# Grouped-query decode attention beside a gated MLP: semaphores by hand, one TensorE loop over the heads, two K/V slots, another order of loads

## The chip, the cores and the metric

The kernel runs on one core of one Trainium2 chip. The metric is the device time of one execution in microseconds (us). Before the change it is 682.59 us, the median of three runs (682.55 to 682.78).

## What is computed

A decode step for 8 sequences of one token. The token is normalised, projected to 32 query heads, and attends over a cache of 4096 keys and values in 8 K/V heads of width 128 (four query heads share one). The result is multiplied by a gate from a small MLP and added to the input. All data are float32.

```
xn = layernorm(x)                                       # x: 8 x 1 x 512
q  = (xn @ wq) as 32 heads of 128
s  = softmax(q k^T / sqrt(128)) v, heads joined, @ wo   # k, v: 8 x 8 x 4096 x 128
z  = gelu(xn @ w_in);  z1, z2 = halves of z
g  = silu((z1 * (layernorm(z2) * w_sp + b_sp)) @ w_out)
out = x + s * g
```

K and V are 134 MB each; wq and wo 8.39 MB each; the MLP's weights 5.57 MB.

## The kernel before

The host lays every tensor out as 128 partitions with long rows. K and V come as 32 tiles of 8.39 MB (128 x 16384 floats): for each of the 8 K/V heads two K tiles and two V tiles, each for four of the eight sequences ("half 0" and "half 1"). All large loads go through one ring of three slots of that size and are issued by SyncE's queue (SP), in program order: the MLP's weights (L59), wq (L74), then per head K half 0 and 1 (L289) and V half 0 and 1 (L296). A load waits until the tile that stood in its slot has been read for the last time, and a waiting load holds up the loads behind it in the queue.

At the start VectorE (DVE) normalises x; TensorE (PE) runs the MLP (L144 to L192, with DVE, ScalarE (ACT) and GpSimd (POOL) steps between, up to the gate at L200), while its weights' slot also holds the MLP's intermediate values; then the projection of the queries in two quads of four heads (L207, L213). DVE copies the queries into qz, zero-padded so that 32 columns of a matmul's weights hold one sequence's four query heads at its own place (L219).

Each head: 64 matmuls of scores (L230), 32 for each K tile, accumulate into one PSUM tile of 128 x 1024. The softmax goes over DVE, ACT and four short PE steps (L237 to L258); its result is transposed on PE (L262) and copied zero-padded to pT in 16 small copies (L266). Then 16 value matmuls for each of four pairs of sequences (L275), two pairs for each V tile; DVE multiplies by a mask and reduces (L278, L280), and PE combines (L284).

The last head differs: its second V tile comes in two pieces, behind 12 of wo's 32 blocks (L319), which go into the ring's third slot, and ahead of six pieces with the other 20 (L322). A block is 128 x 512 floats. Blocks 0 to 27 belong to the first seven heads and are multiplied as early as they land (L304, "folding"), the first 12 between the last head's value matmuls. The last head's four blocks are multiplied directly into the output's layout (L351); the folded sum is copied to SBUF (L343) and joined by 8 matmuls (L359). Two DVE steps (L363, L364) and a store (L365) end the program.

The order is made by the Tile framework: it records every tile's readers and writers, sets semaphores itself, and every engine's instructions are written out one after another, all eight heads in full.

Of the kernel before, what the change touches and what calls it, by code (L numbers as in the profile page):

```python
# [1 line left out]

# [11 lines left out]
P = 128  # L14
# [3 lines left out]
G = 4  # L18
# [8 lines left out]
UNIT = 2 * G * 512  # L27
SLOT = HALF * UNIT
W = 64
OUT_ROWS = 2 * B  # L30
WO_EARLY = 12
WO_PIECES = [(12, 20), (20, 26), (26, 28), (28, 30), (30, 31), (31, 32)]
FOLDED = HKV * REP - REP
AHEAD = FOLDED + 2


@with_exitstack
def tile_gqa_gmlp_decode(ctx: ExitStack, tc: tile.TileContext, x, kT, v, wq, wo, w_mlp, out, gate, stored):
    nc = tc.nc
    head = ctx.enter_context(tc.tile_pool(name="head", bufs=1))  # L40
    l = head.tile([P, HKV], F32, name="l")
    nm = head.tile([P, HKV], F32, name="nm")
    neg_half = head.tile([P, 1], F32, name="neg_half")
    diag = head.tile([P, G], F32, name="diag")
    ring = ctx.enter_context(tc.tile_pool(name="ring", bufs=3))
    const = ctx.enter_context(tc.tile_pool(name="const", bufs=1))
    work = ctx.enter_context(tc.tile_pool(name="work", bufs=1))
    small = ctx.enter_context(tc.tile_pool(name="small", bufs=2))
    ps_fix = ctx.enter_context(tc.tile_pool(name="ps_fix", bufs=1, space=bass.MemoryType.PSUM))
    ps = ctx.enter_context(tc.tile_pool(name="ps", bufs=2, space=bass.MemoryType.PSUM))  # L50

    def slot():
        return ring.tile([P, SLOT], F32, name="slot")


    mlp_slot = slot()
    n_in, n_out = NK * 2 * FH, NB * D
    n_mlp = n_in + n_out + P
    nc.sync.dma_start(mlp_slot[:, :n_mlp], w_mlp)  # L59
    w_in_sb = mlp_slot[:, :n_in].rearrange("p (k n) -> p k n", k=NK)  # L60
    w_out_sb = mlp_slot[:, n_in:n_in + n_out].rearrange("p (j d) -> p j d", j=NB)
    side_sb = mlp_slot[:, n_in + n_out:n_mlp]
    spare = [n_mlp]

    def from_slot(rows, n):
        lo = spare[0]
        spare[0] = lo + n
        return mlp_slot[:rows, lo:lo + n]

    x_sb = from_slot(B, D)  # L70
    nc.scalar.dma_start(x_sb, x)

    wq_sb = slot()
    nc.sync.dma_start(wq_sb, wq)  # L74
    wq_sb = wq_sb.rearrange("p (k n) -> p k n", k=NK)


    ident = const.tile([P, P], F32, name="ident")
    make_identity(nc, ident)
    nc.gpsimd.memset(neg_half, -0.5)  # L80
    xnT = const.tile([P, NK, R], F32, name="xnT")
    nc.gpsimd.memset(xnT, 0.0)
    qz = const.tile([P, HKV, B * R], F32, name="qz")
    nc.gpsimd.memset(qz, 0.0)  # L84
    same = const.tile([P, G, R], F32, name="same")
    nc.vector.tensor_reduce(same[:, 0, :], ident.rearrange("p (g r) -> p r g", g=G),
                            op=ALU.add, axis=AX.X)
    for g in range(1, G):
        nc.vector.tensor_copy(same[:, g, :], same[:, 0, :])
    same_all = same.rearrange("p g r -> p (g r)")  # L90
    nc.vector.tensor_reduce(diag, same[:, 0, :].rearrange("p (e g r) -> p g e r", e=2, g=G),
                            op=ALU.add, axis=AX.XY)
    fold = const.tile([P, 2, REP], F32, name="fold")
    nc.vector.tensor_reduce(fold, same[:, 0, :].rearrange("p (e g r) -> p e r g", e=2, g=G),
                            op=ALU.add, axis=AX.X)
    pT = const.tile([P, J, B, 2, G * REP], F32, name="pT")
    nc.gpsimd.memset(pT, 0.0)  # L97
    pick = const.tile([P, 2, R], F32, name="pick")
    nc.vector.memset(pick, 0.0)
    for a in range(2):  # L100
        nc.vector.tensor_copy(pick[:, a, a * B:(a + 1) * B], same[:, 0, :B])

    sc = ps_fix.tile([P, 2, 512], F32, name="sc")
    o_ps = [ps_fix.tile([P, G, DH], F32, name=f"o_ps{i}") for i in range(2)]
    po_ps = ps_fix.tile([P, 2, B * REP], F32, name="po_ps")
    for t in o_ps:
        nc.vector.memset(t, 0.0)

    def scratch(shape, name):
        t = ps.tile([P, 512], F32, name="scr")  # L110
        n = 1
        for s in shape[1:]:
            n *= s
        return t[:shape[0], :n]


    st = small.tile([B, 6], F32, name="st")
    mv = small.tile([B, 2], F32, name="mv")
    rstd = small.tile([B, 2], F32, name="rstd")
    xn = from_slot(B, D)  # L120
    nc.vector.bn_stats(st, x_sb)
    nc.vector.bn_aggr(mv, st)
    nc.vector.tensor_scalar(rstd[:, 0:1], mv[:, 1:2], EPS, None, op0=ALU.add)
    nc.gpsimd.tensor_tensor(rstd[:, 1:2], rstd[:, 0:1], neg_half[:B, 0:1], op=ALU.pow)
    nc.vector.tensor_scalar(xn, x_sb, mv[:, 0:1], rstd[:, 1:2], op0=ALU.subtract, op1=ALU.mult)
    pt = scratch([P, NK * B], "xnT")
    for k in range(NK):
        nc.tensor.transpose(pt[:, k * B:(k + 1) * B], xn[:, k * P:(k + 1) * P], ident[:B, :B])
# [276 lines left out]
```

## Time and profile before

| what | value |
|---|---|
| median of the runs | 682.59 us (682.55 to 682.78) |
| profiled execution, first to last instruction (span) | 680.7 us |
| the difference, which lies around the span | 1.9 us |
| moved by DMA | 291.18 MB, mean 428 GB/s |
| TensorE matmul busy | 360.8 us, 2488 matmuls |
| VectorE busy | 121.5 us, 376 instructions |
| instruction fetches on queue q8 | 19 packets, 0.31 MB |

How to read a profile: "PE" is TensorE's matmuls, "PEld" its weight loads; a float32 matmul of the program stands in the trace as two matmuls and two weight loads. SPq is SyncE's DMA queue. A row of the timeline is: start in us, duration in us, engine, line, operation, output<-inputs, shape, count, and in brackets how long the engine had been idle and what ended it. A row of the stage table is: stretch, length, busy us (count) of PE, PEld, DVE, ACT and POOL, granted TensorE clock, share of the 16 DMA engines at work, GB/s. A row of the chain is start, length and what the time went to. A row of DMA issues gives the time from issue to landing; where it has no KB, it is a tile of 8.39 MB.

### The profile page before, as it was taken

The page shows a single profiled execution, that of the slowest core. Times are in us where ns is not written, and L with a number is a line of the kernel's source. Part 1 is how long each engine was busy: PE and PEld are TensorE (multiplying, and loading weights), DVE is VectorE, ACT ScalarE, POOL GpSimd, SP SyncE. Part 2 cuts the span into 40 slices and gives each one's busy share as a digit, 9 for nine tenths or more (in the row PEclk, how much of TensorE's full clock was granted, in tenths as well). Part 3 has the DMA queues.
Part 4 walks back from the last instruction along what each step waited for, and adds up shares of the span by engine and source line. Part 5 has one row for each costly group of instructions (what it writes and reads, how often), then busy time and mean ns, then how long its engine had stood idle before and what let it go on. Part 6 is the DMA issues. An engine that isn't in the chain of part 4 may idle for free.

```text
span 680.7 us, 5589 instructions
## 1 busy us (share of the span) xinstructions
PE 360.8 (53%) x2488; PEld 117.0 (17%) x2488; DVE 121.5 (18%) x376; ACT 13.4 (2%) x27; POOL 5.6 (1%) x13
## 2 busy tenths in 40 slices
PE   0465564446565454446654464555654355555667
PEld 0121121112111121112211021111211021111212
DVE  2440041203220032201310032201311032200321
ACT  0000000000000000000000000000000000000000
POOL 2000000000000000000000000000000000000000
PEclk9797666778877666787766678877666787876678
DMA  9999999999999999999999999999999999999996
GB/s 390 431 433 431 432 431 432 435 440 435 448 439 429 431 428 431 431 428 431 432 431 440 439 436 435 428 431 428 435 429 435 443 432 444 435 436 435 405 425 264
DMA packets 6231, 291.18 MB, mean 428 GB/s; under 512 B 824, under 2 KB 824, under 8 KB 1344
## 3 DMA queue, kind: packets, MB, share of 16 engines
q1 hardware_dynamic: 6192, 290.82, 98.8%
q8 instruction: 19, 0.31, 0.2%
q10 hardware_dynamic: 16, 0.02, 0.0%
q14 instruction: 4, 0.03, 0.0%
HBM read 290.80 MB, written 0.03 MB: 427 GB/s over the span
## 4 chain that ended last, share of the span: by engine, by line
DMA 76%; PE 16%; issue 4%; another core or an unknown queue 2%; DVE 1%; POOL 1%; SPq 0%; POOLq 0%; ACT 0%
DMA slot<-in_kT 41%; DMA slot<-in_v 28%; PE sc L230 10%; DMA slot<-in_wo 6%; PE o_ps L275 6%; PE sc L304 0%; POOL qz L84 0%; PE sc L351 0%; POOL pT L97 0%; SPq L296 0%; DVE o_all L343 0%; DVE slot L188 0%; POOLq L399 0%; DVE slot L199 0%
## 5 line engine op out<-in xcount | busy, mean ns | idle before, releaser
L230 PE MATMUL sc<-slot,qz 128*32 128x512 f32 x1024 | 148.4, 745 | 145.0 <-DMA slot<-in_kT 145.0
L275 PE MATMUL o_ps<-slot,pT 128*32 128x512 f32 x1024 | 150.5, 749 | 86.2 <-DMA slot<-in_v 86.2
L230 PEld LDWEIGHTS sc<-slot,qz 128*32 128x32 f32 x1024 | 36.3, 134 | 250.7 <-DMA slot<-in_kT 144.6
L275 PEld LDWEIGHTS o_ps<-slot,pT 128*32 128x32 f32 x1024 | 44.9, 130 | 180.1 <-issue 119.1
L237 DVE TENSOR_REDUCE nm<-sc 128x1 f32<-128x1024 f32 x8 | 9.8, 1225 | 290.1 <-PE sc L230 290.1
L278 DVE TENSOR_TENSOR o_all<-o_ps,diag 128x512 f32<-128x512 f32 x32 | 22.1, 692 | 204.4 <-PE o_ps L275 204.4
L280 DVE TENSOR_REDUCE o_sb<-o_all 128x128 f32<-128x512 f32 x32 | 34.2, 1070 | 1.1
L284 PE MATMUL po_ps<-fold,o_sb 128*128 128x8 f32 x64 | 12.4, 266 | 24.0 <-DVE o_sb L280 24.0
L239 ACT ACTIVATE p<-sc,nm 128x1024 f32<-128x1024 f32 x8 | 8.9, 1114 | 580.2 <-DVE nm L237 580.2
L262 PE MATMUL scr<-ident,p 128*128 128x128 f32 x64 | 14.3, 396 | 10.7 <-DVE p L258 10.7
L266 DVE COPY pT<-scr 128x64 f32<-128x64 f32 x128 | 17.5, 216 | 8.9 <-PE scr L262 8.9
L284 PEld LDWEIGHTS po_ps<-fold,o_sb 128*128 128x128 f32 x64 | 9.5, 188 | 40.9 <-DVE o_sb L280 27.4
L262 PEld LDWEIGHTS scr<-ident,p 128*128 128x128 f32 x64 | 11.3, 204 | 11.1 <-issue 11.1
L144 PE MATMUL scr<-slot,xnT 128*32 128x512 f32 (+1 forms) x32 | 5.2, 750 | 9.6 <-DMA slot<-in_w_mlp 9.6
L304 PE MATMUL sc<-slot,oT 128*8 128x512 f32 x56 | 7.9, 593 | 0.3 <-DMA slot<-in_wo 0.3
L242 PE MATMUL scr<-ident,nm 128*1 128x128 f32 x8 | 2.2, 270 | 10.9 <-DVE nm L237 10.9
L207 PE MATMUL scr<-slot,xnT 128*32 128x512 f32 x64 | 7.3, 594 | 0.0
L255 PE MATMUL scr<-wl,same 128*128 128x1 f32 x16 | 3.4, 284 | 6.2 <-DVE wl L253 6.2
L258 DVE TENSOR_SCALAR p<-p,w 128x1024 f32<-128x1024 f32 x8 | 6.0, 752 | 0.3
L219 DVE COPY qz<-scr 128x4 f32<-128x4 f32 x64 | 4.6, 152 | 1.5 <-PE scr L213 1.5
L159 PE MATMUL scr<-part_sum,same 128*128 128x1 f32 x4 | 1.1, 348 | 7.0 <-DVE part_sum L157 7.0
L248 PE MATMUL scr<-ident,full 1*128 1x1 f32 x8 | 1.5, 189 | 5.7 <-DVE full L246 5.7
(87 smaller groups left out, 62.9 us busy)
## 6 DMA issues: line engine op xcount, KB each, us to landing
slot<-in_v SPq DMA_DIRECT2D x2, 4096.0 KB, 31.5
slot<-in_w_mlp SPq DMA_DIRECT2D x1, 5440.0 KB, 15.4
slot<-in_wo SPq DMA_DIRECT2D x1, 3072.0 KB, 37.6
slot<-in_wo SPq DMA_DIRECT2D x1, 2048.0 KB, 40.5
slot<-in_wo SPq DMA_DIRECT2D x1, 1536.0 KB, 43.9
slot<-in_wo SPq DMA_DIRECT2D x2, 512.0 KB, 44.6
slot<-in_wo SPq DMA_DIRECT2D x2, 256.0 KB, 35.0
slot<-in_kT SPq DMA_DIRECT2D x16, 48.6
```

Source lines behind the costliest of these rows:

```text
L207: nc.tensor.matmul(pq[R * g:R * (g + 1), :], xnT[:, k, :], wq_sb[:, k, lo:lo + REP * DH], start=(k == 0), stop=(k == NK - 1))
L230: nc.tensor.matmul(sc[R * g:R * (g + 1), c, :], qz[:, h, b * R:(b + 1) * R], k_sb[:, i, c, g, :], start=(b == 0), stop=(b == B - 1))
L237: nc.vector.tensor_reduce(m, sc, op=ALU.max, axis=AX.XY, negate=True)
L239: nc.scalar.activation(p.rearrange("p j s -> p (j s)"), sc.rearrange("p c s -> p (c s)"), AF.Exp, bias=m, accum_out=l[:, h:h + 1])
L258: nc.vector.tensor_scalar(p, p, w, None, op0=ALU.mult)
L262: nc.tensor.transpose(t[:, j * P:(j + 1) * P], p[:, 4 * c + j, :], ident)
L266: nc.vector.tensor_copy(pT_v[:, 4 * c + j, :, e, e].rearrange("p i (g r) -> p i g r", g=G), tv[:, :, e])
L275: nc.tensor.matmul(of[R * c:R * (c + 1), :], pT[:, j, 2 * i + e].rearrange("p e q -> p (e q)"), v_pair[:, e, j], start=(j < G and e == 0), ...
L278: nc.vector.tensor_mul(o_all, o, diag[:, :, None].to_broadcast([P, G, DH]))
L280: nc.vector.tensor_reduce(o_sb, o_all.rearrange("p g d -> p d g"), op=ALU.add, axis=AX.X)
L284: nc.tensor.matmul(po[:, i * 2 * REP:(i + 1) * 2 * REP], o_sb, fold.rearrange("p e r -> p (e r)"), start=True, stop=True)
L304: nc.tensor.matmul(part[R * r:R * r + B, :], oT[:, h, r, :], wo_sb[:, m, :], start=(m < REP), stop=(m >= FOLDED - REP))
```

## The change

The kernel is written without the Tile framework. Every wait and every count is set by hand, on one semaphore for each of DVE, ACT, POOL and PE and one for each load. What changes with it:

1. There are two K/V slots in place of a ring of three, `slot_a` for half 0 and `slot_b` for half 1 of both K and V. The third, `slot_c`, holds wq, then the MLP's intermediate values, then wo. `slot_b` holds the MLP's weights first.
2. The order at the start is wq, the MLP's weights, K half 0; and on PE the projection stands ahead of the MLP.
3. PE runs the eight heads as one loop of eight passes (`te.Fori`), whose waits on DVE are a counter, `tokens`, that DVE raises at each handover. The other engines' instructions are written out in full.
4. The query copies are one per quad into `q_all` and one per head into a `qz` of one head. The softmax's copies to pT are four per head.
5. The last V tile is loaded whole, and all of wo comes behind it in six pieces of 18, 8, 2, 2, 1.5 and 0.5 blocks. A folding block is two matmuls of 256 columns in two PSUM banks in place of one of 512, and the copy of the folded sum is split between DVE and ACT.
6. x for the last addition is a load of its own, behind wo.

SP's queue, at the start of the program. Before:

```order
L59 DMA slot<-in_w_mlp 128x10880
L74 DMA slot<-in_wq 128x16384
L289 DMA slot<-in_kT 128x16384
L289 DMA slot<-in_kT 128x16384 [waits DMAHW0_49,DMAHW1_49,DVE_49,PE_49]
L296 DMA slot<-in_v 128x16384 [waits DMAHW2_49,PE_49]
L296 DMA slot<-in_v 128x16384 [waits DMAHW3_49,PE_49]
```

The same place after the change (all loads have the helper's line, 133; `v_done` and `pe_done` are DVE's and PE's counters):

```order
L133 DMA slot<-in_wq 128x16384 [waits barrier_Pool_Activation_PE_DVE_SP_release]
L133 DMA slot<-in_w_mlp 128x10880
L133 DMA slot<-in_kT 128x16384
L133 DMA slot<-in_kT 128x16384 [waits v_done]
L133 DMA slot<-in_v 128x16384 [waits pe_done] x2
```

wq has moved ahead of the MLP's weights; the second K tile waits for DVE, at the MLP's gate, in both, and now goes into the slot of the MLP's weights ahead of any V tile.

PE at the start, before: the MLP's matmuls (L144 to L192) and then the projection (L207, L213).

```order
L159 MATMUL scr<-part_sum,same 128x1 [waits DVE_49,PE_49] x2
L180 MATMUL scr<-ident,slot 128x128 [waits DVE_49]
L180 MATMUL scr<-ident,slot 128x128
L185 MATMUL scr<-slot 32x512 [waits DVE_49] x2
L185 MATMUL scr<-slot 32x512 x5
L192 MATMUL scr<-slot,pick 32x64 [waits DVE_49]
L192 MATMUL scr<-slot,pick 32x64 x7
L207 MATMUL scr<-slot,xnT 32x512 [waits DMAHW2_49,PE_49]
L207 MATMUL scr<-slot,xnT 32x512 x15
L213 MATMUL scr<-ident,q_sb 128x128 [waits DVE_49]
```

After: the projection (L181, L186), and behind it the MLP's first matmul (L217), which waits for the MLP's weights and for a DVE step behind the projection:

```order
L181 MATMUL t<-slot,xnT 32x512 [waits v_done,ld_wq]
L181 MATMUL t<-slot,xnT 32x512 x15
L186 MATMUL t<-ident,q_sb 128x128 [waits v_done]
L186 MATMUL t<-ident,q_sb 128x128 x3
L181 MATMUL t<-slot,xnT 32x512 x16
L186 MATMUL t<-ident,q_sb 128x128 [waits v_done]
L186 MATMUL t<-ident,q_sb 128x128 x3
L217 MATMUL t<-slot,xnT 32x512 [waits v_done,ld_mlp]
```

The projection has moved ahead of the MLP. The MLP's other matmuls stand in the same order as before, and the loop over the heads behind them waits for the gate.

SP's queue at the end of the program, before:

```order
L296 DMA slot<-in_v 128x16384 [waits DMAHW6_49,PE_49]
L319 DMA slot<-in_wo 128x6144 [waits DMAHW7_49,PE_49]
L296 DMA slot<-in_v 128x8192 [waits DMAHW0_49,PE_49]
L296 DMA slot<-in_v 128x8192
L322 DMA slot<-in_wo 128x4096
L322 DMA slot<-in_wo 128x3072
L322 DMA slot<-in_wo 128x1024 x2
```

and after:

```order
L133 DMA slot<-in_v 128x16384 [waits pe_done] x2
L133 DMA slot<-in_wo 128x9216 [waits v_done]
L133 DMA slot<-in_wo 128x4096
L133 DMA slot<-in_wo 128x1024 x2
L133 DMA slot<-in_wo 128x768
L133 DMA slot<-in_wo 128x256
L133 DMA x_out<-in_x_res 128x64
```

wo's first blocks have moved from ahead of the last V tile to behind it.

The diff replaces nearly the whole file; this is its core, with the new functions:

```
-WO_EARLY = 12
-WO_PIECES = [(12, 20), (20, 26), (26, 28), (28, 30), (30, 31), (31, 32)]
+LAST = 31 * D + D // 2
+WO_PIECES = [(0, 18 * D), (18 * D, 26 * D), (26 * D, 28 * D), (28 * D, 30 * D), (30 * D, LAST), (LAST, NWO * D)]
...
+    def op(self, name, *args, after=(), alone=False, **kw):
+        self.wait(*after)
+        ins = getattr(self.engine, name)(*args, **kw)
+        if not alone and self.n:
+            ins._wait_ge(self.sem, self.n)
+        ins.then_inc(self.sem, 1)
+        self.n += 1
+        return self, self.n
...
-    ring = ctx.enter_context(tc.tile_pool(name="ring", bufs=3))
+    slots = [sb(f"slot{i}", [P, SLOT], 512) for i in range(3)]
+    slot_a, slot_b, slot_c = slots
...
+    def load(engine, dst, src, key, *after):
+        for lane, n in after:
+            engine.wait_ge(lane.sem, n)
+        engine.dma_start(dst, src).then_inc(loaded[key], 16)
+    load(nc.scalar, x_sb, x, "x")
+    load(nc.sync, slot_c, wq, "wq")
+    load(nc.sync, slot_b[:, :N_MLP], w_mlp, "mlp")
+    load(nc.sync, slot_a, kT[0, 0], "a")
...
+    STEPS = ["k0", "k1", "a", "mm", "tot", "t0", "t1", "v0", "v1", "c0", "v2", "v3", "c3"]
+    def take():
+        te.wait_ge(tokens, 1).then_inc(tokens, -1)
+    def take_load(key):
+        te.wait_ge(loaded[key], 16).then_inc(loaded[key], -16)
...
+    pe_wait(q_ready, pT_zero)
+    pe_wait(gate_made)
+    with te.Fori(0, HKV):
+        take_load("a")
+        mark(scores(0, slot_a))
+        take_load("b")
+        mark(scores(1, slot_b))
...
+        take()
+        take_load("a")
+        mark(values(0, slot_a))
+        mark(values(1, slot_a))
+        mark(combine(0))
+        take_load("b")
+        mark(values(2, slot_b))
+        combine(1)
+        mark(values(3, slot_b))
+        combine(2)
+        mark(combine(3))
...
+    def give():
+        nc.vector.wait_ge(V.sem, V.n).then_inc(tokens, 1)
...
+    for h in range(HKV):
+        if h:
+            load(nc.sync, slot_a, kT[h, 0], "a", step(h - 1, "c0"))
+            load(nc.sync, slot_b, kT[h, 1], "b", step(h - 1, "c3"))
+        else:
+            load(nc.sync, slot_b, kT[h, 1], "b", gate_made)
+        load(nc.sync, slot_a, v[h, 0], "a", step(h, "k0"))
+        load(nc.sync, slot_b, v[h, 1], "b", step(h, "k1"))
+        softmax(h)
+        for pair in range(B // 2):
+            reduced(h, pair)
...
+    for i, (lo, hi) in enumerate(WO_PIECES):
+        load(nc.sync, slot_c[:, lo:hi], wo[:, lo:hi], f"wo{i}", *([gate_made] if i == 0 else []))
+    load(nc.sync, x_out, x_res, "res")
...
+    for m in range(FOLDED):
+        h, r = divmod(m, REP)
+        need((m + 1) * D)
+        for s in range(2):
+            i = te.matmul(part[s][R * r:R * r + B, :], oT[:, h, r, :], wo_v[:, m, s * D // 2:(s + 1) * D // 2],
+                          start=(m < REP), stop=(m >= FOLDED - REP))
+    copied = [V.op("tensor_copy", part_f[:, :D // 2], part[0], after=[folded]),
+              A.op("activation", part_f[:, D // 2:], part[1], AF.Copy, after=[folded, o_made])]
```

More of the change, by code (lines that the diff above doesn't have):

```diff
@@ L26 @@
 HALF = B // 2
-UNIT = 2 * G * 512
-SLOT = HALF * UNIT
+SLOT = HALF * 2 * G * 512
 W = 64
 OUT_ROWS = 2 * B
-WO_EARLY = 12
-WO_PIECES = [(12, 20), (20, 26), (26, 28), (28, 30), (30, 31), (31, 32)]
[L33 to L44, printed above, removed]
-    ring = ctx.enter_context(tc.tile_pool(name="ring", bufs=3))
[L46 to L87, printed above, removed]
@@ L204, in project_q @@
+    pe_wait(landed("wq"), d)
+    for quad in range(2):
         for k in range(NK):
@@ new lines, in build @@
+    need((FOLDED + 3) * D)
+    direct(FOLDED + 2, range(G))
+    need(LAST)
+    direct(NWO - 1, range(G // 2))
+    need(NWO * D)
+    done = mark(direct(NWO - 1, range(G // 2, G)))
+    V.op("tensor_mul", gate, acc, gate, after=[done])
+    d = V.op("tensor_add", gate, gate, x_out, after=[landed("res")])
+    nc.sync.wait_ge(V.sem, d[1])
+    nc.sync.dma_start(out, gate).then_inc(stored, 16)
+    used = [tokens, *loaded.values(), V.sem, A.sem, L.sem, pe_sem]
+    lo, hi = min(s.num for s in used), max(s.num for s in used)
```

537 lines of the change are left out of this document (286 added, 251 removed).

## The prediction

> **What bounds the kernel now.** I read the page first: the busy shares, the 40 slices, the queues, the chain that ended last.
>
> ```profile
> span 680.7 us, 5589 instructions
> PE 360.8 (53%) x2488; PEld 117.0 (17%) x2488; DVE 121.5 (18%) x376; ACT 13.4 (2%) x27; POOL 5.6 (1%) x13
> ...
> GB/s 390 431 433 431 432 431 432 435 440 435 448 439 429 431 428 431 431 428 431 432 431 440 439 436 435 428 431 428 435 429 435 443 432 444 435 436 435 405 425 264
> ...
> q1 hardware_dynamic: 6192, 290.82, 98.8%
> q8 instruction: 19, 0.31, 0.2%
> ...
> DMA 76%; PE 16%; issue 4%; another core or an unknown queue 2%; DVE 1%; POOL 1%; SPq 0%; POOLq 0%; ACT 0%
> ```
>
> TensorE (PE) works half the span, the DMA engines all of it: 290.82 MB of tensors pass through them. Only the first slice and the last three are below their usual rate. A stage table of the steady part gives that rate:
>
> ```profile
> 54.00:650.00 596.00, 320.08 (x2153) 103.41 (x2157) 96.41 (x259) 11.27 (x24) 0.00 (x0) 0.73 1.00 434
> ```
>
> 434 GB/s, the engines full. 290.82 MB at 434 are 670.1 us, so of the 680.7 only 10.6 us are open to any change: the start, the end, and whatever single DMA engines lose. Since a transfer is spread over 16 engines, the slowest one sets every landing. The end shows what that costs:
>
> ```profile
> 672.00:673.00 1.00, 0.88 (x8) 0.41 (x8) 0.36 (x3) 0.00 (x0) 0.00 (x0) 1.00 0.90 363
> 673.00:674.00 1.00, 0.71 (x10) 0.12 (x8) 0.00 (x0) 0.00 (x0) 0.00 (x0) 1.00 0.56 229
> ...
> 675.00:676.00 1.00, 1.00 (x8) 0.09 (x4) 0.00 (x0) 0.00 (x0) 0.00 (x0) 1.00 0.39 152
> ```
>
> The last number but one is the share of engines at work: 0.90, 0.56, and 0.39 two slices on. Some engines are done at 672.5, others work on for 4 us, with nothing to do for the rest. Where do they fall behind? The chain in order of time gives the landings of K tiles three loads apart:
>
> ```profile
> 39.78 35.54 DMA slot<-in_kT
> ...
> 512.04 47.94 DMA slot<-in_v
> ...
> 560.11 9.90 PE o_ps L275 x64
> ...
> 570.03 49.06 DMA slot<-in_kT
> ```
>
> Landings at 75.32 (39.78 + 35.54), 559.98 and 619.09: 559.98 to 619.09 is 59.1 us, while three loads of 8.39 MB at 434 are 58.0. So a load loses about 1.1 us now and then. The instruction queue offers the cause: 0.2% of 16 engines x 680.7 is 21.8 us for 19 fetches, 1.1 us each on one engine (0.9 to 1.4 with the rounding). I take it that an engine that carries a fetch is 1.1 us late from then on, and that the slowest was hit about three times.
>
> **The change, part by part.**
>
> *Start.* Before, the MLP weights come first, then wq. Their landings after issue (the DMA view), their issues (the timeline of the DMA queue), and the MLP's and the projection's rows in the timeline of all engines:
>
> ```profile
> slot<-in_w_mlp SPq DMA_DIRECT2D x1, 5440.0 KB, 15.4
> slot<-in_wq SPq DMA_DIRECT2D x1, 34.3
> ```
>
> ```profile
> 0.74 0.36 SPq L59 DMA_DIRECT2D slot<-in_w_mlp  x1
> 1.16 0.42 SPq L74 DMA_DIRECT2D slot<-in_wq  x1
> ```
>
> ```profile
> 6.13 0.48 DVE L137 MEMSET scr<- 128x512 f32 x1
> ...
> 16.29 5.23 PE L144 MATMUL scr<-slot,xnT 128*32 128x512 f32 x32 [9.63 <-DMA slot<-in_w_mlp]
> ...
> 21.59 0.69 DVE L147 COPY slot<-scr 128x512 f32<-128x512 f32 x1 [5.21 <-PE scr L144]
> ...
> 32.89 3.85 PE L185 MATMUL scr<-slot 128*32 128x512 f32 x14 [0.17 <-DVE slot L181]
> ...
> 39.48 0.22 DVE L200 TENSOR_TENSOR gate<-scr,slot 128x64 f32<-128x64 f32 x1
> ...
> 42.84 3.64 PE L207 MATMUL scr<-slot,xnT 128*32 128x512 f32 x32
> ...
> 47.29 0.66 PE L213 MATMUL scr<-ident,q_sb 128*128 128x128 f32 x4 [0.81 <-DVE q_sb L210]
> ```
>
> The MLP's weights land at 0.74 + 15.4 = 16.1, its gate stands at 39.70, and K half 1, which reuses that slot, is issued at 39.78, far ahead of the landing of K half 0, which is 8.39 MB behind wq's at 35.5 (1.16 + 34.3): 54.8. The queue never empties. Now wq is first: it lands 2.82 MB later than the MLP's weights did, 16.1 + 6.5 = 22.6. The projection's first quad on a cold PE takes 5.2 (L144's row), its scaling and transposes 47.95 - 46.48 = 1.5; the second, warm, 47.95 - 42.84 = 5.1; then two short copies and the 0.48 memset, 0.9: 35.3. The MLP's weights land at 35.5 (same bytes as before). Its 32 matmuls run warm, 3.6 (L207's row); then the chain from L147 to the gate, 39.70 - 21.59 = 18.1; a joined hT copy and separate wait instructions, not shown in the trace, 0 to 0.6, I take 0.3. Gate at 57.5. But now K half 1 waits for that gate with *nothing behind K half 0 in the queue*: the other slot holds K half 0, the third MLP scratch. The engines run dry near 54. K half 1 lands at 57.6 + 2.6 (15.4 less 5.57 MB at 434) + 19.3 = 79.5, against 75.3: **+4.2**. If PE is cold for the first matmuls as it was at L144, +5.8; if the seven matmuls of L185, cold before (3.85), run warm (1.9), +2.3.
>
> *The heads.* Two slots in place of three: each load is issued when the tile before in its slot is read, while the other slot's load is in flight. The chain's row of 9.90 for two value pairs (scores are alike) against 19.3 per load leaves 9.4 us between a freed slot and the dry queue; where the slot waits for the last combine (about 2.3 more, rows of the tail below), 7. The softmax must fit between the scores and the next V landing, 9.4; nothing there gets longer but some wait instructions, while 16 pT copies become 4. So 0, covered by 7 us; a wait would have to grow by that much to cost anything.
>
> *The loop and its fetches.* Rows of the page, per head an eighth:
>
> ```profile
> L230 PE MATMUL sc<-slot,qz 128*32 128x512 f32 x1024 | 148.4, 745 | 145.0 <-DMA slot<-in_kT 145.0
> L275 PE MATMUL o_ps<-slot,pT 128*32 128x512 f32 x1024 | 150.5, 749 | 86.2 <-DMA slot<-in_v 86.2
> L284 PE MATMUL po_ps<-fold,o_sb 128*128 128x8 f32 x64 | 12.4, 266 | 24.0 <-DVE o_sb L280 24.0
> L262 PE MATMUL scr<-ident,p 128*128 128x128 f32 x64 | 14.3, 396 | 10.7 <-DVE p L258 10.7
> ```
>
> 128 + 128 + 8 + 8 and four small ones are 276 matmuls, with their weight loads 552 instructions a head. 4976 in all for 19 fetches is one fetch per 262. The looped program has about 1,200: 552 in the body, 560 outside, and 112 more since the folding matmuls are halved. If the body stays where TensorE reads it, 4 or 5 fetches are left, on different engines: one delay of 1.1 instead of about three. From K half 1 at 79.5, 260.1 MB at 434 are 599.3: 678.8, plus 1.1: the last byte at 679.9. Before: 75.3 + 599.3 = 674.6 against the real 677.4 (below), so 2.8 were lost after 75.3 and **-1.7** is what the loop brings. From both sides: no delay at all, -2.8; more fetches than now, rivals 2 and 3.
>
> [...]
>
> *Tail.* Now V's last tile comes whole, then 8.39 MB of wo. Rows of the tail before: the view of the line that issues wo's pieces (shortest, median and longest issue in ns, first and last start), and the DMA view cut to the last of them.
>
> ```profile
> L322 SPq DMA_DIRECT2D slot<-in_wo x6: 328/421/432, 629.4 to 645.7; - x6
> ```
>
> ```profile
> slot<-in_wo SPq DMA_DIRECT2D x1, 256.0 KB, 31.7
> ```
>
> ```profile
> 648.69 2.76 PE L304 MATMUL sc<-slot,oT 128*8 128x512 f32 x24
> ...
> 670.30 0.69 DVE L278 TENSOR_TENSOR o_all<-o_ps,diag 128x512 f32<-128x512 f32 x1 [6.48 <-PE o_ps L275]
> 671.02 1.05 DVE L280 TENSOR_REDUCE o_sb<-o_all 128x128 f32<-128x512 f32 x1
> 672.12 0.39 PE L284 MATMUL po_ps<-fold,o_sb 128*128 128x8 f32 x2 [0.25 <-DVE o_sb L280]
> 672.55 0.29 DVE L339 COPY oT_last<-po_ps 128x32 f32<-128x32 f32 x2 [0.48 <-PE po_ps L284]
> ...
> 677.52 0.64 PE L351 MATMUL sc<-slot,oT_last 128*16 128x64 f32 x32
> 678.22 0.23 DVE L363 TENSOR_TENSOR gate<-sc,gate 128x64 f32<-128x64 f32 x1 [1.47 <-PE sc L351]
> ```
>
> Before, the last piece lands at 645.7 + 31.7 = 677.4 and the final multiply starts 0.8 later. Now, from V's landing: its two value pairs 9.9, reduce, combine and copy as from 670.30 to 672.84, 2.5; then all 28 folding blocks, which could not start earlier, 6.2 (12 took 2.76; half as wide and twice as many is the same); the two half copies on DVE and ACT 0.5 (a whole one took 0.69, as L147's row), beside the first direct blocks 0.7; eight matmuls on the copies and the last two blocks 0.9 (16 take 0.64); 0.5 for the handovers: the multiply starts 20.7 after V. The last wo piece lands 8.39 MB / 434 + 0.3 for small pieces = 19.6 after V. So it starts 1.1 after the last byte instead of 0.8: +0.3. Against it, no closing barrier of the framework, unknown, between 0 and the 0.5 that the span leaves after the store; I take -0.2. Tail **+0.1**: 680.7 - 677.4 = 3.3 becomes 3.4.
>
> Sum: 4.2 - 1.7 + 0.1 = +2.6 on the span, 683.3. Around the span lie 682.6 - 680.7 = 1.9 (median of the runs less span): **685.2 us**.
>
> **Rivals.** A difference of 0.2%, 1.4 us, is about what a measurement of this kernel tells from none.
>
> 1. *The gate chain is quicker (not slower).* If PE runs warm at all steps between wq and the gate, L185's kind included, K half 1 goes out near 55.7: +2.3 instead of +4.2, 683.3; with the whole barrier gone too, 683. For it: PE works more densely than before at that place. Against: L185 was cold with matmuls 0.2 us ahead of it. It decides from a gate before 56.2. For *faster*, the gate would have to stand by 53.5, and 35.5 + 3.6 + 16.2 forbids that; only loss of all fetch delays and a shorter tail together reach 681.
> 2. *The loop saves no fetch.* At each jump back TensorE fetches the body again, 2 to 3 blocks a pass, 19 to 25 in all, spread as now: three or four delays on the worst engine, 3.9 instead of 1.1: 688.0. The wait at the jump itself costs nothing up to 7 us, since K is still in flight. For it: the trace has a fetch per 262 instructions all along, so nothing is shown to be kept. Against: nothing jumps in it.
> 3. *The same engine each pass.* As 2, but each block of the body always on its own engine: eight delays, 9 us: 693. Nothing in the trace speaks for it but that two fetches may meet on one engine.
>
> **How the numbers follow.** Forecast 685.2 with 0.46; rival 1 0.16; rival 2 0.24; rival 3 0.07; something faster than 681.2, by all small bounds at once, 0.07. Range 682.4 to 689.5: it leaves the fast corner (0.09) and rival 3 with some of 2 (0.10). Faster by over 0.2%: 0.07. Within: rival 1 and the low end of the forecast (warm and no delay at all), 0.18. Slower: 0.75.
>
> **What would show it.** Start: the DMA slices empty for about 4 us between 54 and 60, K half 1 issued near 57.6, TensorE's L290 of the new kernel starting there. Loop: the instruction queue's count, 4 to 6 in the forecast, 19 or more in rivals 2 and 3; the engines' end less ragged than 0.90, 0.56, 0.39. Heads: scores and values still wait for DMA at every tile; if instead DMA slices fall below 9 in the middle, the 7 us were not enough and I am wrong there. Tail: final multiply about 1 us after the last wo landing. I am wrong altogether if the gate stands before 54, or if the rate in the middle is not 434.

## The result, and the profile after

The changed kernel takes **687.70 us** (median of four runs, 687.01 to 688.54), beside 682.63 (682.55 to 682.78) for the kernel before on the same chip. The ratio is 1.0074, with a 95% interval from 1.0059 to 1.0088: 5.1 us slower. The profiled execution took 687.01 us with a span of 685.7, so 1.3 us lie around its span, where there were 1.9 before; it was the shortest of the four runs, 0.7 below the median.

The page of the changed kernel: busy time, rates of the 40 slices, and DMA queues (packets, MB, share of 16 engines).

```profile
span 685.7 us, 5749 instructions
...
PE 361.2 (53%) x2544; PEld 124.2 (18%) x2544; DVE 113.7 (17%) x222; ACT 13.8 (2%) x28; POOL 4.2 (1%) x13
...
GB/s 418 398 433 264 460 432 425 428 428 432 428 432 428 428 428 459 443 432 428 432 432 428 432 428 428 451 447 436 428 432 429 428 432 432 428 440 459 436 397 293
...
q1 hardware_dynamic: 6048, 290.85, 98.2%
q8 instruction: 5, 0.08, 0.0%
q14 instruction: 3, 0.02, 0.0%
```

The same bytes pass, and TensorE is as busy as before. Two things stand out. The fourth slice moves 264 GB/s, where before it moved 431; with slices of 17.1 us that is (431 - 264) / 431 x 17.1 = 6.6 us of lost transfer. And queue q8 has 5 packets in place of 19, at 42, 85, 112, 680 and 683 us: the loop is fetched once and then stays.

**The hole.** The start in the timeline of all engines: start, duration, what, and in brackets the idle time ahead and what ended it.

```profile
22.55 6.53 PE L181 MATMUL t<-slot,xnT 128*32 128x512 f32 x32 [14.41 <-DMA slot<-in_wq]
...
30.56 3.64 PE L181 MATMUL t<-slot,xnT 128*32 128x512 f32 x32
...
36.54 0.48 DVE L48 MEMSET t<- 128x512 f32 x1 [0.18 <-DVE qz L48]
37.17 3.63 PE L217 MATMUL t<-slot,xnT 128*32 128x512 f32 x32 [1.42 <-DVE t L48]
40.94 0.69 DVE L48 COPY slot<-t 128x512 f32<-128x512 f32 x1 [3.91 <-PE t L217]
...
59.23 0.23 DVE L48 TENSOR_TENSOR gate<-misc,slot 128x64 f32<-128x64 f32 x1
59.49 0.33 SPq L133 DMA_DIRECT2D slot<-in_kT  x1
59.81 4.55 PE L290 MATMUL sc<-slot,qz 128*32 128x512 f32 x28 [2.24 <-PEq L282]
```

The gate stands at 59.46, and K half 1 is issued behind it, 19.7 us later than before. The stage table of the same stretch (the last two numbers are the share of the DMA engines at work and GB/s):

```profile
52.00:54.00 2.00, 1.41 (x10) 0.44 (x11) 0.42 (x1) 0.00 (x0) 0.00 (x0) 0.50 0.09 33
54.00:56.00 2.00, 2.00 (x10) 0.21 (x3) 0.00 (x0) 0.00 (x0) 0.00 (x0) 0.57 0.00 0
56.00:58.00 2.00, 0.65 (x19) 0.29 (x16) 0.92 (x2) 0.00 (x0) 0.00 (x0) 1.00 0.00 0
58.00:60.00 2.00, 0.19 (x4) 0.22 (x8) 0.97 (x3) 0.26 (x1) 0.00 (x0) 0.79 0.02 4
60.00:62.00 2.00, 2.00 (x12) 0.45 (x9) 0.00 (x0) 0.00 (x0) 0.00 (x0) 0.50 1.58 524
```

From 52 to 60 this table has next to nothing moving. It counts transfers in lumps (in the kernel before, where there is no hole, its slice from 52 to 54 has 164 GB/s between two of 426 and 492), so the length of the hole is better read from landings: the first of the 16 DMA engines to finish its part of K half 0 did so at 54.16, the first to finish its part of K half 1 at 80.70, 26.5 us later, where a tile takes 19.3: 7.2 us without work. Behind it the engines are full for good, as the two long rows of the same table show:

```profile
160.00:400.00 240.00, 134.29 (x880) 44.67 (x884) 35.90 (x66) 4.22 (x9) 0.00 (x0) 0.71 1.01 435
400.00:640.00 240.00, 126.54 (x850) 43.17 (x843) 38.99 (x74) 5.63 (x12) 0.00 (x0) 0.73 1.00 434
```

**The end.** The timeline of the last steps:

```profile
682.38 0.64 PE L429 MATMUL sc<-slot,oT_last 128*16 128x64 f32 x31
683.17 0.23 DVE L48 TENSOR_TENSOR gate<-sc,gate 128x64 f32<-128x64 f32 x1 [1.12 <-PE sc L429]
...
683.68 0.35 SPq L452 DMA_DIRECT2D out<-gate  x1
```

The trace also records, for every load, when each of the 16 DMA engines finished its part. The first and the last of the 16 say more than the last alone, and the comparisons below rest on them ("spread" is the distance between the two; "start back" is the kernel with the start as before, in the profile of experiment 5):

| | before | after | start back |
|---|---|---|---|
| K half 1, first engine, us | 73.65 | 80.70 | 73.53 |
| K half 1, last engine | 75.32 | 81.24 | 75.16 |
| last piece of wo, last engine | 677.41 | 682.25 | 675.64 |
| spread at that piece or the one before it | 4.65 | 1.83 | 3.00 |
| final multiplication starts | 678.22 | 683.17 | 677.03 |
| span | 680.7 | 685.7 | 679.2 |

### The profile page after: what moved, and what is told of

Its sections match the earlier page's. It is cut to its first block, busy times and chain, and to the rows that moved or that the text cites. A ratio compares the mean times of both kernels' runs of the same rounds, so it can differ in the third digit from the quotient of the medians.

```text
span 685.7 us, 5749 instructions
## 1 busy us (share of the span) xinstructions
PE 361.2 (53%) x2544; PEld 124.2 (18%) x2544; DVE 113.7 (17%) x222; ACT 13.8 (2%) x28; POOL 4.2 (1%) x13
## 5 line engine op out<-in xcount | busy, mean ns | idle before, releaser
L290 PEld LDWEIGHTS sc<-slot,qz 128*32 128x32 f32 x1024 | 40.5, 133 | 234.0 <-issue 234.0
L325 PE MATMUL t<-ident,p 128*128 128x128 f32 x64 | 15.5, 424 | 11.7 <-PEq L279 11.7
L306 PE MATMUL po<-fold,o_sb 128*128 128x8 f32 x64 | 12.4, 266 | 14.2 <-PEq L279 14.2
L181 PE MATMUL t<-slot,xnT 128*32 128x512 f32 x64 | 10.2, 792 | 14.4 <-DMA slot<-in_wq 14.4
L306 PEld LDWEIGHTS po<-fold,o_sb 128*128 128x128 f32 x64 | 9.7, 190 | 35.8 <-issue 35.8
L325 PEld LDWEIGHTS t<-ident,p 128*128 128x128 f32 x64 | 12.6, 224 | 12.1 <-issue 12.1
L48 DVE COPY pT<-t 128x256 f32<-128x256 f32 x32 | 12.1, 419 | 12.0 <-PE t L325 11.2
L321 PE MATMUL misc<-wl,same 128*128 128x1 f32 x16 | 3.8, 310 | 8.2 <-PEq L279 8.2
L181 PEld LDWEIGHTS t<-slot,xnT 128*32 128x32 f32 x64 | 2.3, 137 | 20.4 <-DMA slot<-in_wq 14.5
L321 PEld LDWEIGHTS misc<-wl,same 128*128 128x128 f32 x16 | 3.4, 265 | 8.7 <-issue 8.7
```

The costliest lines, as they stand in the source:

```text
L48: ins = getattr(self.engine, name)(*args, **kw)
L181: i = te.matmul(t[0][R * g:R * (g + 1), :], xnT[:, k, :], wq_v[:, k, lo:lo + REP * DH], start=(k == 0), stop=(k == NK - 1))
L290: i = te.matmul(sc[R * g:R * (g + 1), c, :], qz[:, b * R:(b + 1) * R], k_v[:, n, c, g, :], start=(b == 0), stop=(b == B - 1))
L306: return te.matmul(po[:, pair * 2 * REP:(pair + 1) * 2 * REP], o_sb[pair % 2], fold.rearrange("p e r -> p (e r)"), start=True, stop=True)
L321: mark(te.matmul(misc[:, 320:321], same_all, one["wl"], start=True, stop=True))
L325: i = te.transpose(t[c][:, j * P:(j + 1) * P], p[:, 4 * c + j, :], ident)
```

## The experiments

"Before" in a ratio is the kernel before, run on the same chip between the runs. Eleven runs, of ten kernels (1 and 5 are the same one), in three groups: the hole at the start, the loop, and what is left at the end. Labels count in the order of the runs.

**1. The start put back.** The MLP's weights are loaded and used ahead of wq; its intermediate values lie behind them in the same slot; wo waits for the projection instead of the gate (the last pair of lines below shows only the end of that line). Loop, two slots and tail stay as changed.

```
-    load(nc.sync, slot_c, wq, "wq")
     load(nc.sync, slot_b[:, :N_MLP], w_mlp, "mlp")
+    load(nc.sync, slot_c, wq, "wq")
...
-    spare = [0]
+    spare = [N_MLP]
...
-        return slot_c[:, lo:lo + n]
+        return slot_b[:, lo:lo + n]
...
-*([gate_made] if i == 0 else [])
+*([wq_read] if i == 0 else [])
```

> The changed kernel with the start put back: the MLP's weights first, then wq, and the MLP ahead of the projection; the MLP's intermediate values lie behind its weights in the slot, so wo's slot waits only for the projection. Theory (the gap at the start is what costs): the gate stands near 40 us, the second K tile is queued long before the first lands, no empty DMA slices; the second K tile lands at about 75.3 instead of 81.2, and the time falls by 5.2 to 5.9 us from 687.7, to 682 (681.5 to 682.5), with the span's tail and the 5 fetches unchanged. Rival (two slots, not the start, lose the time, spread over the heads): the second K tile lands at 75, but the end moves by under 2 us, 686 or more.

Measured: 680.95 us (679.84 to 684.21), ratio 0.9977 [0.9967, 0.9988]. No slice is near 264 any more. That is below the expected range: the start costs even more, 6.8 us against the change, not the 5.7 by which 682 lay under it.

**2. The loop undone**, the rest as changed.

```
-    with te.Fori(0, HKV):
+    for _ in range(HKV):
```

> The changed kernel with the eight heads written out on TensorE instead of the loop, all else the same. Theory (the loop saves instruction fetches, which delay single DMA engines): about 20 fetches instead of 5, the engines' end more ragged, the last wo piece 1 to 2 us later, time 688.7 to 689.7. Rival (the loop saves nothing or its jumps cost): same time within 0.5 us, or faster than 687.2.

Measured: 690.18 us (688.79 to 694.28), ratio 1.0116 [1.0095, 1.0137], 2.5 us above the change. Its instruction queue:

```profile
q8 instruction: 20, 0.33, 0.2%
```

The spread at the end is 4.58 instead of 1.83 us, and the last piece of wo lands at 685.14, 2.9 us later; its first engine is done at 680.56, in the change at 680.42. So what is lost is spread alone. The time lies above the expected range: the loop saves rather more than the 1.7 us that the prediction credited it with.

**3. K half 1 issued a little earlier**: it waits for the MLP's last read of its weights, not for the gate.

```
-            load(nc.sync, slot_b, kT[h, 1], "b", gate_made)
+            load(nc.sync, slot_b, kT[h, 1], "b", mlp_read)
```

> The changed kernel, in which the load of the second K tile waits for the last matmul that reads the MLP's weights instead of for the finished gate. In the trace of the changed kernel that is 56.2 instead of 59.5. Theory (each us of that wait is a us of empty DMA and of time): the load goes out 3.2 us earlier, time 684.5 (684.0 to 685.0). Rival (the gap is partly covered, or the slots lose the time): a gain under 1.5 us.

Measured: 684.96 us (684.32 to 685.70), ratio 1.0035 [1.0022, 1.0048]. The issue in its timeline:

```profile
56.41 0.33 SPq L133 DMA_DIRECT2D slot<-in_kT  x1
```

That is 3.1 us earlier than 59.49, and the time falls by 2.7, within the expected range. A shorter wait makes a shorter hole and a shorter time.

**4. TensorE kept busy ahead of wq**, by 12 idle matmuls, so that the projection runs at full clock.

```
-    pe_wait(landed("wq"), d)
+    pe_wait(d, pT_zero)
+    for _ in range(12):
+        te.matmul(po, ident, pT.rearrange("p j b e q -> p (j b e q)")[:, :512], start=True, stop=True)
+    pe_wait(landed("wq"))
```

> The changed kernel with twelve matmuls without use (identity by zeros into an idle PSUM bank) on TensorE while it waits for wq, so that the projection starts on a warm clock. Theory: the first quad takes 3.7 us instead of 6.5, the MLP starts at its weights' landing, 35.4 instead of 37.2, and the gate and the second K tile come 1.7 us earlier: time 686.0 (685.4 to 686.6). If the seven matmuls of the MLP's second product also find a warm clock, another 1.5. Rival (the clock at the start has no part in the loss): same time within 0.4.

Measured: 687.63 us (686.93 to 688.11), ratio 1.0070 [1.0057, 1.0083]: nothing gained, which is the rival's time. Its timeline tells why:

```profile
22.80 3.64 PE L184 MATMUL t<-slot,xnT 128*32 128x512 f32 x32 [1.53 <-DMA slot<-in_wq]
...
35.60 5.33 PE L220 MATMUL t<-slot,xnT 128*32 128x512 f32 x32 [2.51 <-DMA slot<-in_w_mlp]
...
59.70 0.22 DVE L48 TENSOR_TENSOR gate<-misc,slot 128x64 f32<-128x64 f32 x1
```

and the stage table has the granted clock (third number from the end) behind the wait:

```profile
36.00:40.00 4.00, 4.00 (x29) 1.11 (x23) 0.00 (x0) 0.00 (x0) 0.00 (x0) 0.61 1.15 496
```

The first quad is indeed 2.9 us shorter. But then TensorE waits 2.5 us for the MLP's weights, which land only now, and its clock falls (0.61 from 36 to 40): the MLP's first matmuls take 5.33 instead of 3.63. The gate stands 0.46 us *later* than in the change. As long as wq is ahead in the queue, the MLP can't start before 35.6, whatever TensorE does.

**5. The start put back, once more**, beside 6 to 8, for its median and its spread.

> The kernel with the start put back, run once more beside the next ones, for its median and above all for its spread. Its profiled run before had the last piece of wo at 675.3 but the last multiplication only at 680.1, and TensorE's clock in between at 0.54 and 0.61 (668 to 676). Theory A, TensorE's clock sets this kernel's end: the times spread again over 3 us or more (679.8 to 684), median near 681. Theory B, that was one odd run: spread under 1.5 us, median near 680.5, and the profile has the last multiplication about 1 us behind the last piece of wo.

Measured: 680.54 us (680.08 to 684.38), ratio 0.9983 [0.9969, 0.9997]. Ten runs, seven from 680.08 to 680.74 and three at 682.74, 683.80 and 684.38. Two profiled executions of this one kernel caught both sides. In the stage table of the one of 683.70 us (experiment 1):

```profile
668.00:672.00 4.00, 3.24 (x30) 1.64 (x34) 0.41 (x3) 0.00 (x0) 0.00 (x0) 0.54 0.97 401
672.00:676.00 4.00, 4.00 (x52) 1.64 (x47) 0.00 (x0) 0.00 (x0) 0.00 (x0) 0.61 0.32 115
```

and of the one of 680.54 us:

```profile
668.00:672.00 4.00, 3.29 (x58) 2.04 (x62) 0.36 (x3) 0.00 (x0) 0.00 (x0) 1.00 0.96 396
672.00:676.00 4.00, 3.78 (x97) 2.25 (x87) 0.42 (x1) 0.38 (x1) 0.00 (x0) 1.00 0.30 108
```

The DMA engines do the same in both. TensorE had the folding blocks to do, at a granted clock of 0.54 and 0.61 in the one and 1.00 in the other, and did 82 against 155 matmuls in those 8 us. The final multiplication stood at 680.14 and 677.03. With the hole gone, TensorE's clock in the tail can set the end. So neither theory holds as a whole: the typical run is B's, and three of ten are A's. Of the longer times only the 683.70 of experiment 1 has a profile; that the clock made the others too is argued.

**6 and 9. TensorE kept busy in the tail**: idle matmuls in every pass, 20 and then 14, in the 10 us in which TensorE waits for V half 1.

```
         mark(combine(0))
+        for _ in range(20):
+            te.matmul(po[:, 128:512], ident, pT.rearrange("p j b e q -> p (j b e q)")[:, :384], start=True, stop=True)
         take_load("b")
```

> Start put back, and 20 idle matmuls of 384 columns in each pass ahead of the wait for V's second half, where TensorE stands still for some 10 us; their result is read by nobody. Theory A (TensorE's clock sets the end once the gap is gone): TensorE is warm when V lands, its four groups of 32 take about 1.84 us a group of 16 at full clock, the tail from V's landing shrinks from 24.4 to about 17 us, and the last piece of wo sets the end: last multiplication 1 us behind it, 680.3 (679.8 to 680.8), spread under 1.5 us. Rival: the clock is taken away whatever TensorE did before, or the extra work costs clock: median 681 or more with the same spread of 3 us.

Measured with 20: 681.06 us (680.48 to 683.16), ratio 0.9979 [0.9970, 0.9987], above the expected range. The last pass in its timeline:

```profile
649.67 9.52 PE L333 MATMUL po<-pT,ident 128*128 128x384 f32 x29
659.12 3.68 PE L300 MATMUL o_ps<-slot,pT 128*32 128x512 f32 x32
```

All value matmuls run at full clock now (3.68 for 32), but the idle ones last beyond V's landing at 656.0, and what the clock gave is lost again.

> Start put back, and 14 idle matmuls in each pass ahead of the wait for V's second half instead of 20. With 20 they had run until 659.1, 3 us past V's landing, and ate what the full clock gave (four groups of 16 in 3.68 and 3.68 instead of 6.01 and 3.68 us a pair). With 14, at 0.66 us each, they end about 655.2, just before V lands at 656.1. Theory A: the last multiplication comes about 2.4 us sooner on TensorE's side, so the last piece of wo sets the end; 0.4 us under the kernel with the start put back on its typical run, 680.2 (679.8 to 680.7), and no run above 682. Rival, the clock falls again in the tail whatever went ahead: some runs at 682 to 684 as in the kernel with the start put back.

Measured with 14: 680.54 us (679.89 to 681.17), ratio 0.9968 [0.9956, 0.9980].

```profile
646.46 9.28 PE L333 MATMUL po<-pT,ident 128*128 128x384 f32 x28
656.11 3.68 PE L300 MATMUL o_ps<-slot,pT 128*32 128x512 f32 x32 [0.38 <-PEq L282]
```

The median is that of experiment 5, which fits a typical run that wo's last piece had already set; but none of the six runs is above 681.2, and the final multiplication stands 0.71 us behind wo's last landing (675.51). It is 2.3 us faster than the kernel before. That times above 682.4 are gone is likely, not shown: they are 7 of 22 in experiments 1 and 5, and at that rate six runs would have none one time in ten.

**7. Start put back and loop undone**: the edits of 1 and 2 together. What is left of the change is two slots, hand-set semaphores and the tail.

> Start put back and the loop undone, everything else as in the change. If what the loop saves (15 of 20 instruction fetches) is worth the same without the gap at the start, the time is 2.5 us above the kernel with the start put back, 683.4 (682.5 to 684.3), about the time of the kernel before, with about 20 fetches and the last landings 4 to 5 us apart. If the loop's worth came only with the gap, 681.

Measured: 682.35 us (681.49 to 683.05), ratio 0.9995 [0.9986, 1.0004], with 20 fetches: 1.8 us above experiment 5, just under the expected range, and not to be told from the kernel before.

**8. Four heads in the loop's body, two passes.**

```
-    with te.Fori(0, HKV):
+    with te.Fori(0, HKV // 4):
+        for _ in range(4):
```

> The change, with four heads written out in the loop's body and two passes, so that the body is about nine blocks of 16 KB instead of about two and a half. [...] By a store that holds the whole body: 11 or 12 fetches, 688.5 (687.9 to 689.2). [...]

Measured: 689.98 us (689.10 to 690.63), ratio 1.0105 [1.0091, 1.0120], in the 689.3 to 690.7 that had been expected, with about 20 fetches, if the second pass fetches everything again; K half 1 at 81.25 to 81.81, and

```profile
q8 instruction: 22, 0.36, 0.2%
```

20 fetches for the 5200 TensorE instructions that experiment 2's trace holds are one per 260; the 552 of a head are thus some two blocks, those of four heads some nine. The body of two blocks stays (5 packets in the change); that of nine is fetched again in the second pass (22), and then the loop costs as much as no loop (689.98 beside the 690.18 of experiment 2).

**10 and 11. VectorE's fetches.** In every kernel with one head in the loop's body the spread stays flat behind the first pass, but for one or two steps: in that of experiment 9 from 1.48 to 1.88 us at the landing that starts at 286 us, and from 1.76 to 2.73 at 518. The second instruction queue, q14, has packets at 282 and 512 us. To see whose they are, VectorE got 90 more instructions a head, waits that are satisfied long before; first in all heads, then not in the last one.

```
         for pair in range(B // 2):
             reduced(h, pair)
+        for _ in range(90 if h < HKV - 1 else 0):
+            nc.vector.wait_ge(V.sem, 1)
```

> The kernel with the start put back and 14 idle matmuls, and 90 waits that are long satisfied at the end of each head on VectorE, where it stands still for scores anyway. In the profiles of the looped kernels the distance between the first and the last DMA engine's landing jumps only twice after the first pass, at 286 and 518 us (1.48 to 1.88, 1.76 to 2.73 us), 2 to 5 us after the two packets of the second instruction queue (q14, at 282 and 512). Theory: these are VectorE's own instruction fetches, one per three heads, and they cost a DMA engine some 1 us each like TensorE's. With 90 more instructions a head there are 5 to 8 packets on q14 instead of 3, the distance at the end grows from 2.6 to 3.5 or more, and the time from 680.5 to 681.5 (680.8 to 682.8). Rival, q14 belongs to another engine or its packets cost nothing: 3 packets, distance 2.6, 680.5.

Measured: 688.01 us (686.60 to 688.58), ratio 1.0074 [1.0060, 1.0088], far beyond both. Most of that was the edit's own doing: in the last head the waits themselves stood on the way to the end.

```profile
672.81 0.29 DVE L48 COPY oT_last<-po 128x32 f32<-128x32 f32 x2 [4.63 <-issue]
673.15 1.06 PE L421 MATMUL sc<-slot,oT 128*8 128x256 f32 x8 [4.41 <-DVE oT_last L48]
```

> As the kernel with 90 waits a head, but without them in the last head, where they stood on the way to the end: 4.6 us ahead of the last copy of po, and TensorE cold for its first 40 matmuls behind them. The second instruction queue had 6 packets there, and the distance between the engines' landings grew by 0.96 to 0.99 us at four of them, one upon the other, as if all hit the same DMA engine. Theory: 6 packets again (5 if the last falls away), distance at the end 4.4 to 5.4 instead of 2.6, the last piece of wo at 677 to 678 instead of 675.5, and the time 682.5 (681.8 to 683.2), 2 us more than with 14 idle matmuls alone. Rival, the 688 came from the waits themselves and the fetches cost the end nothing: 680.5.

Measured: 682.90 us (682.57 to 684.24), ratio 1.0004 [0.9995, 1.0013], 2.4 us above experiment 9.

```profile
q8 instruction: 5, 0.08, 0.0%
...
q14 instruction: 6, 0.05, 0.0%
```

Six packets, at 56.5, 204.7, 287.6, 418.9, 518.8 and 640.4 us, and the spread steps up at 286 (1.79 to 2.75), 421 (2.62 to 3.56), 518 (3.49 to 4.41) and 653 (4.32 to 5.30). Four times 0.92 to 0.98, one upon the other, which only one and the same engine can give. The first engine's part of wo's last piece lands at 672.84, in experiment 9 at 672.91, so the waits delayed nothing but that engine. q14 is VectorE's, and four of its six fetches hit the engine that is already last.

## Why the prediction was right, and where it was off

The forecast, 685.2 us and slower by more than 0.2%, had sign and mechanism right; the time, 687.7, lies in its range (682.4 to 689.5), 2.5 us above. The sum on the span came out at +5.0 (685.7 - 680.7) where it said +2.6. The 1.9 us around the span, carried over from the kernel before, were 1.3 here, 0.6 too many; that covered part of the miss in the start, and is luck.

**The bound.** Right (the landing at 559.98, which the prediction calls a K tile's, is a V tile's; the tiles are of one size, so its sum holds). 434 and 435 GB/s in the long rows after; only the start and the slowest DMA engine's end were open.

**The start, +4.2.** Right in its chain, too small in its size; this is the term that was mis-sized. The last engine's landing of K half 1 moved by 5.9 (81.24 - 75.32). The 1.7 that are missing there arose ahead of the MLP, which started at 37.17, not at 35.5: 1.3 in the first quad, 6.53 in place of the 5.2 taken from another cold group, the rest in the small steps behind it. From there to the gate it took 22.29 where 22.0 had been worked out. The +5.8 that the prediction gave for a cold PE is near 5.9 only by luck: it meant the MLP's matmuls, and these ran in 3.63. The experiments put a larger price still on the start: 687.70 - 680.95 = 6.8 and 687.70 - 680.54 = 7.2. That is the first engine's shift, 80.70 - 73.53 = 7.2, not the last one's. The two kernels without a loop say the same: 690.18 - 682.35 = 7.8, first engine 81.38 - 73.56 = 7.8, last one 81.83 - 75.17 = 6.7. In experiment 3, between the two, the first engine is 3.1 earlier than in the change (77.60), the last one 2.4 (78.88), the time 2.7. The spread shows what happens. At K half 0 it is 2.13 in the changed kernel; across the hole it falls to 0.54, since late engines finish while early ones have nothing to do; one and two tiles on it is back at 1.62 and 2.10, the loop's two fetches at 85 and 112 lying between; that they are the cause is read from their times alone. In experiment 4 such a fetch, at 69, fell into K half 1 itself, which has a spread of 1.92 there and lands at 83.06, 1.8 later than in the change, and the whole is no slower (687.63). So the hole's levelling looked like a gain of 1.1 us and was lost again within 40 us. By landings of the last engine alone, the prediction could not see it.

**The heads, 0.** Right. Experiment 7 holds the two slots, the own semaphores and the new tail without start and loop: 682.35 against 682.55, -0.2 (0.9986 to 1.0004 of before). From K half 1's last landing to wo's it takes 602.07 (677.24 - 75.17), the kernel before 602.09. No slice in the middle falls.

**The loop, -1.7.** Right: five fetches, as forecast, worth 1.8 (682.35 - 680.54, experiments 7 and 5) or 2.5 (690.18 - 687.70, experiment 2 and the change). In the prediction's own count, from K half 1's last landing, it shows as -1.1 only (682.25 - 81.24 = 601.0 against 602.1), since that count gives the levelling to the start. By that count 1.7 us were lost behind K half 1 (601.0 - 599.3), where one delay of 1.1 was forecast: the fetches at 85 and 112, and a step of the spread from 1.65 to 1.95 at 526, behind a fetch of VectorE's at 524. VectorE's fetches were left out of the prediction. Nor was the slowest engine hit three times for 1.1 before: behind K half 1 the spread grows from 1.67 to 4.58, by 1.2 and 1.1 at two landings and by small steps for the rest. That a head's body stays where TensorE reads it was an assumption of the prediction, which the profile before did not show. The runs show it: 552 instructions at 260 a block are a little over two blocks, eight passes that kept nothing would fetch sixteen or more, and q8 has 5 packets in all. Experiment 8's body of about nine blocks did not stay (22 packets). No run lies between, so how long a body may be is not measured.

**The tail, +0.1.** Right. The multiplication stands 20.5 us behind V's last landing (683.17 - 662.71; forecast 20.7) and 0.9 behind wo's (forecast 1.1); 3.45 us from there to the end, forecast 3.4. What it did not see is how close TensorE's side and wo's are, so that a lower clock there moved the final multiplication by 3.1 us between two profiled executions of one kernel (680.14 and 677.03, experiment 5).

**The rivals.** Rival 1, a quicker gate, is out: the gate stood 2.0 later, not sooner (59.46 against 57.5), the MLP's second product, cold before with 3.85, took 3.32 and not the 1.9 that the prediction estimated for a warm one, and experiment 4 shows why nothing on TensorE brings it before the MLP's weights. Rival 2, a loop that saves no fetch, gave 688.0, nearest to the time of all cases; its mechanism is refuted by 5 packets and by experiment 2. The time alone would have picked the wrong cause. Rival 3 is out for TensorE; what it described, each fetch on the same DMA engine, is what four of VectorE's six did in experiment 11.

Taken one after another, the parts are 682.55 before, -0.2 for slots, semaphores and tail, -1.8 for the loop, +7.2 for the start: 687.7. Each is a difference of two of these medians, so that they add up is no test; in another order the loop is worth 2.5 and the start 7.8. The runs were on several chips, on which the kernel before took 682.55 to 682.86.

## What to carry to other kernels

When a slot's last reader is late, ask what else stands in the DMA queue behind the load that waits: with the MLP's weights first in the queue the wait was free, with two slots as well (experiment 1); with wq first it emptied the queue, and that is paid by the time in which the first engine stood idle (7.2 us here), even if the engines come out of it level. On a kernel that is bound by DMA, count every engine's instruction bytes: a loop whose body stays takes TensorE's fetches away (here 5 packets in place of 20, and 22 with a body four times as long), and the code written out on the other engines then sets what is left (four of VectorE's packets added 0.92 to 0.98 us each in experiment 11). Once such a bound is lifted by a few us, look at the next one before measuring on: here TensorE's clock in the last 20 us, which moved the final multiplication by 3.1 us.

## What the runs showed of the hardware

*An instruction fetch slows one DMA engine.* In experiment 11 four packets of VectorE's (0.05 MB in 6, some 8 KB each) added 0.92 to 0.98 us each on the slowest engine and took the spread from 1.79 to 5.30. The trace has each of these packets at only 0.31 us; why the engine loses three times that stays open. TensorE's, twice the size (0.33 MB in 20), spread better: 20 of them, beside VectorE's three, leave a spread of 4.3 to 4.6 us. In the four traces with 19 to 22 of them, the two largest steps of the spread behind the first head are 0.8 to 1.4 us and come eight fetches apart: behind the 9th and 17th in the kernel before (1.93 to 3.10, 3.37 to 4.51) and experiment 7, behind the 10th and 18th in experiments 2 and 8.

*TensorE's clock.* After a long wait the first matmuls run at half speed (in the change, those of the first quad start four by four 0.85 us apart, those of the second 0.43), but how long varies: 32 of the projection took 6.53 us in the change, 5.9 of it slow (from 22.55 to the first clock record of that trace, a rise at 28.42), and the idle ones of experiment 4 were at full speed after 4.5 (8.50 to a rise at 12.96). Ahead of the first record the profile's clock column reads 1.00 and doesn't show it; the stage table of the change, in which the last three numbers are granted clock, DMA share and GB/s:

```profile
24.00:28.00 4.00, 4.00 (x24) 0.96 (x20) 0.00 (x0) 0.00 (x0) 0.00 (x0) 1.00 0.80 348
28.00:32.00 4.00, 3.10 (x28) 0.96 (x24) 0.98 (x2) 0.00 (x0) 0.00 (x0) 1.00 1.21 522
```

Clock 1.00 in both, 24 matmuls in 4.00 us in the one and 28 in 3.10 in the other. And a clock once granted can go within a short pause: in the profile of experiment 1 the value matmuls ran 32 in 3.68, TensorE then stood still for 1.8 us and went on at half speed, the folding's groups of eight at 1.06 instead of 0.64, each some 0.85 behind the one before instead of 0.43, for almost 6 us:

```profile
662.54 3.68 PE L300 MATMUL o_ps<-slot,pT 128*32 128x512 f32 x32
...
668.32 0.57 PE L306 MATMUL po<-fold,o_sb 128*128 128x8 f32 x2 [1.78 <-PEq L279]
...
669.33 1.06 PE L417 MATMUL sc<-slot,oT 128*8 128x256 f32 x8 [0.44 <-DVE oT_last L48]
```

The changes of the granted clock lie on a grid: in all thirteen traces, every stretch between two of them is a whole multiple of 3.41 us. The slow 5.9 us fit it. Counted back from the rise at 28.42, the change's trace has marks of that grid at 25.01 and 21.59; the projection, from 22.55, started 0.95 us into the interval between them, and only the next one, to 28.42, was busy throughout. The two sides of experiment 5 fit as well. In experiment 1's profile an interval ended at 668.31, the pause of 1.78 us, from 666.54, lay in it whole, and the clock fell. In experiment 5's the same pause, 666.50 to 668.27, lay across the end of an interval at 667.88, and the clock stayed. Over the thirteen traces, 414 of the 415 falls follow an interval in which TensorE's matmuls and weight loads filled half the time or less, and all 409 rises one in which they filled 79% or more (not every such interval is followed by a change). What decides, the traces don't show.
